# A 1-core attention and squared-ReLU FFN kernel: six blocks of weights stored whole and split later, and the engine order of c21 and c22 in the joint blocks

## Chip, core and metric

The kernel runs on one core of a Trainium2 chip. The metric is the device time of one execution in microseconds (us), the median over the runs shown. The engines are called by the profile's names: PE (TensorE), PEld (its weight loads), DVE (VectorE), ACT (ScalarE), POOL (GpSimd), SP (SyncE, which issues nearly all DMAs here).

## The reference, cut to what matters

```python
# attention, 8 x 8 heads, 576 rows, head_dim 64
q_s = softmax of q over its last axis;  k_s = softmax of k over the sequence
kv  = einsum('bhsd,bhde...', k_s, v);   attn = einsum(q_s, kv)
x   = attn.transpose(0, 2, 1, 3).reshape(4608, 512)
h   = np.maximum(x @ w_in, 0.0)          # w_in  512 x 2048
out = (h * h) @ w_out                    # w_out 2048 x 512
```

The FFN is most of the work. Its operands are split into a high and a low fp32r part, and each product is made of three matmuls (high x high, high x low, low x high).

## The kernel before, in words

The 4608 rows are nine tiles of 512 columns of x. Tiles 0 to 4 are the main part: for each of 16 slices f of w_in a first product, relu and square, a split, and a second product two slices later. The attention of later batches runs between them.

The last four tiles are done as two **joint blocks** (k = 0 and 1) of two tiles each, by a Strassen-Winograd scheme with seven products where there would be eight. `first_products(k)` loops over n = 0..7, the eight pairs of w_in slices. Each pair of slices is four quadrants a11, a12, a21, a22 of 128 x 256 values per k-half, and the scheme also needs four sums: s1 = a21 + a22, s2 = s1 - a11, s3 = a11 - a21, s4 = a12 - s2. PE does, for pair n, in this order: P1 (a11) into bank A, P2 (a12) into bank B, then P4 (a22) and P3 (s4) of the pair before (`old`), then P6 (s2) into A, P5 (s1) into B, P7 (s3) into A. Each of these is six matmuls. The two banks alternate between two sets from pair to pair, so P1 of pair n+1 writes the bank that P4 of pair n-1 filled.

What follows each product: u1 (a copy of A by ACT) after P1; c11 = B + u1, relu and square (DVE) after P2; c21 = relu and square of A (ACT) after P4; c12 = B + u2 (DVE), relu and square (ACT) after P3; u2 (ACT) after P6; u3 (ACT) after P7 and then c22 = B + u3 (DVE), relu and square (ACT in the kernel before). The four c go to DRAM (`g_b`), 256 KB each, and come back as operands of `second_products(k)`.

The weights of pair n+1 lie in one of two places, used in turn (`w` for even n, `ring` for odd n). Pairs 0 and 1 are loaded from DRAM with their sums (`w_sums`, high and low parts, 256 KB for each of the seven blocks). For pairs 2 to 7 (`OWN` = 2) the kernel before loads a11, a12 and a22 as high and low parts (three loads of 256 KB by `load_weights`) and beside them `own_a` (512 KB: a22 and a21, high and low), and `own_sums(n, w, step)` makes the four sums on DVE and splits them, in six steps spread over pair n-1. For pair 2 `own_a` is two tiles, own_k and own_q. In the main part `begin_sums(j)` stores the parts of these pairs to `w_sums` straight from where they lie (four DMAs of 256 KB per pair).

The order of the instructions in the joint blocks is that of the code; every engine and the SP queue take theirs in that order. In joint block 1 SP also carries the stores of block 0's output (`out_dram<-o`, four pieces of 64 KB in 128-byte rows each, after a 32 x 32 transpose on DVE). Their tiles o and the tiles of c21 share one pool tag, "gh", with two buffers.

Of the kernel before, what the change touches and what calls it, by code (L numbers as in the profile page):

```python
# [10 lines left out]
F32 = mybir.dt.float32  # L11
# [4 lines left out]
AF = mybir.ActivationFunctionType  # L16
ALU = mybir.AluOpType
# [319 lines left out]
def attention_ffn(  # L337
# [784 lines left out]

    def begin_sums(j):

        one, two = slabs[2 * j], slabs[2 * j + 1]
        for at, slab, cols in (
            (2, one, slice(0, HM)), (6, one, slice(HM, M)), (10, two, slice(HM, M)),
            (12, two, slice(0, HM)),
        )[:3 if j < OWN else 4]:
            Y.dma_start(out=w_sums[j][:, at:at + 2, :], in_=slab[:, :, cols].bitcast(F32))  # L1130

    def sums_by(key):

# [82 lines left out]

    def load_weights(n, w, *names):

        for name in names if w else ():
            if n >= OWN and name in SUMS:  # L1220
                continue
            at = SOURCE[name]
            Y.dma_start(out=w[name].bitcast(F32), in_=w_sums[n][:, at:at + 2, :])

    def own_sums(n, w, step):

        if n < OWN or n >= PAIRS:
            return
        if step == 0:
            if n == OWN:  # L1230
                a = [att.tile([P, 2, HM], F32, tag=tag, name=f"own_{tag}_{n}") for tag in "kq"]
                for i, one in enumerate(a):
                    Y.dma_start(out=one, in_=w_sums[n][:, 10 + 2 * i:12 + 2 * i, :])
            else:
                a = cvt.tile([P, 4, HM], F32, tag="w", name=f"own_a_{n}")
                Y.dma_start(out=a, in_=w_sums[n][:, 10:14, :])
            made["own", n] = [a]
            return
        if step == 1:
            made["own", n] += [cvt.tile([P, 4, HM], F32, tag="w", name=f"own_s_{n}")]  # L1240
        a, s = made["own", n]

        def two(name):
            return w[name][:, 0, :], w[name][:, 1, :]

        def split(name, of):
            S.copy(out=two(name)[0], in_=of)

        def rest(name, of):
            hi, lo = two(name)  # L1250
            V.tensor_tensor(out=lo, in0=of, in1=hi, op=ALU.subtract)

        def put(out, in0, op, in1):
            V.tensor_tensor(out=out, in0=in0, in1=in1, op=op)

        if n == OWN:
            a22, a11, a21, a12 = (a[i // 2][:, i % 2, :] for i in range(4))
        else:
            a22, a11, a21, a12 = (a[:, i, :] for i in range(4))
        s2, s3, s4 = (s[:, i, :] for i in range(3))  # L1260
        if step == 1 and n == OWN:
            put(a22, a22, ALU.add, a11)
            put(a21, a21, ALU.add, a12)
        elif step == 1:
            put(a[:, 0:4:2, :], a[:, 0:4:2, :], ALU.add, a[:, 1:4:2, :])
        elif step == 2 and n == OWN:
            for i, one in enumerate((a11, a12)):
                put(one, w["all"][:, 2 + 4 * i, :], ALU.add, w["all"][:, 3 + 4 * i, :])
        elif step == 2:
            put(a[:, 1:4:2, :], w["all"][:, 2:8:4, :], ALU.add, w["all"][:, 3:8:4, :])  # L1270
        elif step == 3:
            put(a22, a22, ALU.add, a21)
            split("s1", a22)
            if n == OWN:
                put(s2, a22, ALU.subtract, a11)
                put(s3, a11, ALU.subtract, a21)
            else:
                put(s[:, 0:2, :], a[:, 0:2, :], ALU.subtract, a[:, 1:3, :])
        elif step == 4:
            put(s4, a12, ALU.subtract, s2)  # L1280
            rest("s1", a22)
        elif step == 5:
            for name, of in (("s2", s2), ("s3", s3), ("s4", s4)):
                split(name, of)
            rest("s2", s2)
        elif step == 6:
            rest("s3", s3)
            rest("s4", s4)
# [264 lines left out]
    def sums_step(t, f):  # L1553

        j, i = divmod(f, NF // 2)
        j += 2 * (t - 1)
        if t >= 1 and j < NF // 2 and i == 3:
            begin_sums(j)
        for key, at in SUMS_AT.get(t, ()):
            for work, when in zip((full_sums, all_sums, rest_sums), at):  # L1560
                if f == when and f:
                    work(key)
# [16 lines left out]

    THRICE = (0, 0, 2), (4, 5, 7), (9, 10, 12)  # L1580
    SUMS_AT = {t: list(zip(KEYS[3 * t - 3:3 * t], THRICE)) for t in range(1, WT)}
    assert len(KEYS) <= 3 * (WT - 1)

    x_of, w_of, now = {}, {}, {"k": 0}
    ON_POOL = (
# [177 lines left out]
    def pair_p7(z):  # L1763
        product(z.A, z.w["s3"], x_of["t3"], False)
        u3 = temp("xh3", f"u3_{z.n}")
        S.copy(out=u3, in_=z.A)
        c = temp("ek", f"c22_{z.n}", att, 2)
        V.tensor_tensor(out=c, in0=z.B, in1=u3, op=ALU.add)
        own_sums(z.n + 1, w_of.get(z.n + 1), 5)
        S.activation(out=c, in_=c, func=AF.Relu)  # L1770
        square(c, S)
        keep("b21", z.n, c)

    def pair_p4(z):
        product(z.A, z.w["a22"], x_of["t4"], False)
        c = ffn.tile([P, M], F32, tag="gh", name=f"c21_{z.n}")
        S.activation(out=c, in_=z.A, func=AF.Relu)
        square(c, S)
        keep("b22", z.n, c)
# [196 lines left out]
    def first_products(k):  # L1976

        old = None
        for n in range(PAIRS):
            if n == 0 and k == 0:  # L1980
                split_x_of("t4")
                unit(3)
            elif n == 0:
                begin_ring()
            z = pair_begin(n)
            pair_p1(z)
            if n != 1 and turned_late:
                turned_late.pop(0)()
            if n == PAIRS - 1:
                load_raw("b11", 1, raw_place("b11"))  # L1990
            own_sums(n, z.w, 6)
            pair_p2(z)
            if n == 0 and turned_late:
                turned_late.pop(0)()
            if n == PAIRS - 1 and k == 0:
                full_sums(late_key)
            if n == 0 and k == 0:
                unit(2)
                begin_ring()
            elif n == 0:  # L2000
                split_x_of("t4")
                split_x_of("b22")
            if old:
                pair_p4(old)
                load_weights(n + 1, w_of.get(n + 1), "a22")
                own_sums(n + 1, w_of.get(n + 1), 1)
                pair_p3(old)
                load_weights(n + 1, w_of.get(n + 1), "s4")
            own_sums(n + 1, w_of.get(n + 1), 2)
            if n == PAIRS - 1:  # L2010
                load_raw("b11", 2, raw_place("b21"))
                split_step(0)
            pair_p6(z)
            if old:
                pair_c12(old)
            own_sums(n + 1, w_of.get(n + 1), 3)
            if n == 0:
                unit(3)
            pair_p5(z)
            own_sums(n + 1, w_of.get(n + 1), 4)  # L2020
            if n:
                own_sums(n + 2, None, 0)
            if n + 2 < PAIRS:
                w_of[n + 2] = weights(n + 2)
                load_weights(n + 2, w_of[n + 2], "a11", "a12", "s2", "s1")
            elif n == PAIRS - 1:
                if k == 0:
                    for i in range(4):
                        add_sums(late_key, i)
                load_raw("b21", 0, raw_place("t2"))  # L2030
                load_raw("b21", 1, raw_place("t2", 1))
                raw_x = att.tile([P, 4, M], F32, tag="x_next", name=f"raw_b12_{k}")
                for j in range(2):
                    load_raw("b12", j, raw_x[:, 2 * j:2 * j + 2, :])
                split_step(1)
            pair_p7(z)
            load_weights(n + 2, w_of.get(n + 2), "s3")
            if n == PAIRS - 3:
                load_raw("b11", 0, *(temp("v", f"raw_b11_{k}_{i}", att, 2) for i in range(2)))
            for j in FIRST_S[k].get(n, ()):  # L2040
                load_s("s1", j)
            if n == PAIRS - 1:
                for j in range(2):
                    load_raw("b22", j, raw_place("t3", j))
            old = z
        return old

    def second_products(k, old):
# [15 lines left out]
        for m in range(2):  # L2064
            product_step(0, m)
        pair_p4(old)
        load_raw("b12", 2, temp("k", f"raw_b12_{k}_4", att), temp("q", f"raw_b12_{k}_5", att))
        pair_p3(old)
        split_step(3)
# [127 lines left out]
```

## Time and profile before

| what | us |
|---|---|
| median of 3 runs | 837.98 |
| the three runs | 839.4, 836.86, 837.98 |
| the profiled execution | 836.44 |
| its span, first to last instruction | 834.7 |
| PE busy | 819.8 (98%) |
| DVE, ACT, POOL busy | 606.1, 494.6, 139.0 |
| granted TensorE clock, mean | 1.000 |

The table is read like this: PE is busy for all but 14.9 us of the span. The profile's start and end, before the first product and behind the last one, hold most of that; the rest is in single gaps.

### The profile page before, as it was taken

To read this page: it belongs to the slowest core of one execution; us is meant where nothing else is said; L and a number is where in the kernel's file an instruction comes from. 1 tells how busy PE (TensorE), PEld (TensorE's weight loads), DVE (VectorE), ACT (ScalarE), POOL (GpSimd) and SP (SyncE) were. 2 spreads that over 40 slices of the span, in tenths; PEclk is the share of its full clock that TensorE was granted. 3 is DMA by queue.
4 is the path that set the end of the run, shared out by engine and by line. 5 is a ranking of instruction groups with operands and counts; after the bars stand their busy time and mean duration, and the time that the engine had idled before them with its cause. 6 is when DMAs were issued, how large, how long until landed. Compare 5 with 4: busy or idle time off the path is not lost.

```text
span 834.7 us, 12955 instructions
## 1 busy us (share of the span) xinstructions
PE 819.8 (98%) x4411; PEld 663.3 (79%) x4411; DVE 606.1 (73%) x1100; ACT 494.6 (59%) x890; POOL 139.0 (17%) x151
## 2 busy tenths in 40 slices
PE   8999999999999999999999999999999999999997
PEld 7677777888878888888888888888888877787886
DVE  6988976877667755867555775567799966765995
ACT  5988844565655554655555656567744555675442
POOL 5889990001001000001000000000300000000000
PEclk9999999999999999999999999999999999999999
DMA  9993114536436555555637353998866688989455
GB/s 281 371 345 120 39 27 134 134 105 166 109 110 161 132 198 132 163 158 142 168 120 193 69 159 121 313 318 288 326 211 199 184 253 279 272 281 387 133 177 98
DMA packets 230146, 158.08 MB, mean 189 GB/s; under 512 B 147392, under 2 KB 200128, under 8 KB 230080
## 3 DMA queue, kind: packets, MB, share of 16 engines
q1 hardware_dynamic: 224160, 155.55, 61.1%
q10 hardware_dynamic: 5920, 1.71, 0.9%
q8 instruction: 35, 0.57, 0.3%
q14 instruction: 31, 0.25, 0.1%
HBM read 106.95 MB, written 49.81 MB: 188 GB/s over the span
## 4 chain that ended last, share of the span: by engine, by line
PE 80%; DMA 10%; DVE 4%; SPq 3%; ACT 2%; issue 1%; POOL 0%; DVEq 0%; ACTq 0%; POOLq 0%
PE acc L100 24%; PE h L100 21%; PE out L1866 16%; PE h L1315 13%; SPq L100 3%; DMA ring<-w_sums 2%; PE h_kv L100 2%; DMA raw<-in_moe_w_out_dram 2%; DMA k<-in_k_dram 2%; PE x L100 2%; DMA out_dram<-o 1%; DMA w<-g_b 1%; DMA own_a<-w_sums 1%; ACT r L100 1%; DVE w L100 0%
## 5 line engine op out<-in xcount | busy, mean ns | idle before, releaser
L100 PE MATMUL h<-xh,w 128*128 128x512 f32 x632 | 208.6, 392 | 1.0 <-ACT xh L100 0.8
L100 PE MATMUL acc<-w,gh 128*128 128x512 f32 x632 | 197.0, 393 | 0.0
L1866 PE MATMUL out<-w,w 128*128 128x512 f32 x636 | 148.9, 389 | 0.0
L100 PEld LDWEIGHTS h<-xh,w 128*128 128x128 f32 x632 | 118.6, 188 | 27.8 <-ACT xh L100 1.3
L1866 PEld LDWEIGHTS out<-w,w 128*128 128x128 f32 x636 | 119.2, 188 | 25.2 <-DVE w L100 0.4
L100 PEld LDWEIGHTS acc<-w,gh 128*128 128x128 f32 x632 | 117.0, 188 | 25.9 <-issue 1.7
L100 PE MATMUL acc<-w,gl 128*128 128x512 f32 x316 | 123.1, 390 | 0.0
L100 PE MATMUL h<-xl,w 128*128 128x512 f32 x316 | 123.1, 389 | 0.0
L100 DVE TENSOR_TENSOR gl<-r,gh 128x512 fp32r<-128x512 f32 x64 | 44.1, 688 | 82.3 <-ACT gh L100 82.0
L100 ACT ACTIVATE r<-h 128x512 f32<-128x512 f32 x79 | 47.1, 597 | 87.5 <-PE h L100 87.4
L100 POOL PARTITION_ALL_REDUCE kmx<-km x24 | 22.4, 933 | 340.8 <-DVE km L100 340.8
L1315 PE MATMUL h<-w,w 128*128 128x512 f32 x288 | 69.9, 391 | 1.3 <-DMA w<-w_sums 1.3
L100 PEld LDWEIGHTS h<-xl,w 128*128 128x128 f32 x316 | 59.4, 188 | 12.5 <-DVE xl L100 0.4
L100 PEld LDWEIGHTS acc<-w,gl 128*128 128x128 f32 x316 | 59.3, 188 | 12.5
L1315 PEld LDWEIGHTS h<-w,w 128*128 128x128 f32 x288 | 53.7, 188 | 14.0 <-DMA w<-w_sums 2.2
L100 ACT ACTIVATE c<-c 128x512 f32<-128x512 f32 x76 | 48.1, 633 | 19.5 <-DVE c L100 17.9
L100 ACT CAST gh<-r 128x512 fp32r<-128x512 f32 x64 | 39.5, 617 | 21.3 <-PE acc L100 20.8
L100 ACT CAST w<-w 128x1024 fp32r<-128x1024 f32 (+1 forms) x38 | 38.0, 1004 | 18.2 <-PE out L1866 8.6
L1315 PE MATMUL h<-w,ring 128*128 128x512 f32 x192 | 46.7, 391 | 0.4 <-DMA ring<-w_sums 0.4
L100 DVE TENSOR_TENSOR c<-h,u 128x512 f32<-128x512 f32 x48 | 33.0, 687 | 16.9 <-ACT u L100 13.7
L1315 PEld LDWEIGHTS h<-w,ring 128*128 128x128 f32 x192 | 35.8, 188 | 8.9 <-DMA ring<-w_sums 0.6
L100 POOL TENSOR_TENSOR w<-w,raw 128x512 int32<-128x512 int32 x32 | 41.8, 1326 | 1.7 <-DVE w L100 1.1
(238 smaller groups left out, 1266.1 us busy)
## 6 DMA issues: line engine op xcount, KB each, us to landing
w<-wo_sums SPq DMA_DIRECT2D x64, 256.0 KB, 3.4
g_b<-c SPq DMA_DIRECT2D x60, 256.0 KB, 4.4
w<-g_b SPq DMA_DIRECT2D x18, 512.0 KB, 7.1
raw<-in_moe_w_in_dram SPq DMA_DIRECT2D x16, 512.0 KB, 8.2
raw<-in_moe_w_out_dram SPq DMA_DIRECT2D x16, 512.0 KB, 8.8
w<-w_sums SPq DMA_DIRECT2D x32, 256.0 KB, 4.9
w_sums<-w SPq DMA_DIRECT2D x30, 256.0 KB, 2.7
v<-in_v_dram SPq DMA_DIRECT2D x56, 128.0 KB, 2.9
```

What stands on the lines that cost most here:

```text
L100: getattr(self.eng, op)(*map(real, args), **{k: real(a) for k, a in kwargs.items()})
L1315: nc.tensor.matmul(out=out.real(), lhsT=a[:, k * P:(k + 1) * P].real(), rhs=m[k].real(), start=(begin and k == 0 and i == 0), stop=(k == 1 ...
L1866: nc.tensor.matmul(out=banks[name][m].real(), lhsT=a[:, m * P:(m + 1) * P].real(), rhs=b[:, i, :].real(), start=fresh and j == i == k == 0 ...
```

## The change

Three things are changed.

1. For pairs 2 to 7 the main part now adds high and low parts on DVE (`full_sums`, two adds of 128 x 512 per pair) and `whole_sums` stores the sum, the whole float32 values of the four quadrants, with one DMA of 512 KB. In the joint blocks only `own_a` (512 KB: a11, a12 | a21, a22) is loaded; a11, a12 and a22 are split there, a11 and a12 in one ACT cast and one DVE subtraction (step 3), a22 with s1 (step 4). The four sums are made in steps 1 and 2, behind P3.
2. c22's relu and square is one DVE instruction (`SCALAR_TENSOR_TENSOR`) where it was two on ACT, and stands ahead of step 5's splits.
3. `pair_c21` is cut off `pair_p4` and stands behind u2 (behind P6 of the next pair); in the last pair `split_step(1)` stands behind P7 and its u3.

```diff
+    def whole_sums(j):
+        full_sums(("i", j))
+        whole = made.pop(("full", ("i", j)))
+        Y.dma_start(out=w_sums[j][:, 0:4, :], in_=whole.rearrange("p i (c n) -> p (i c) n", n=HM))
...
-        for name in names if w else ():
-            if n >= OWN and name in SUMS:
-                continue
+        for name in names if w and n < OWN else ():
...
-                a = cvt.tile([P, 4, HM], F32, tag="w", name=f"own_a_{n}")
-                Y.dma_start(out=a, in_=w_sums[n][:, 10:14, :])
+                whole = cvt.tile([P, 4, HM], F32, tag="w", name=f"own_a_{n}")
+                Y.dma_start(out=whole, in_=w_sums[n][:, 0:4, :])
...
+        if step == 1:
+            put(s1, a21, ALU.add, a22)
         elif step == 2:
+            put(s2, s1, ALU.subtract, a11)
+            put(s3, a11, ALU.subtract, a21)
+            put(s4, a12, ALU.subtract, s2)
         elif step == 3:
+            S.copy(out=two[0], in_=row)
+            put(two[1], row, ALU.subtract, two[0])
         elif step == 4:
+            split("s1", s1)
+            split("a22", a22)
+            rest("s1", s1)
+            rest("a22", a22)
...
+    WHOLE_AT = {1: [(2, 14)], 2: [(3, 14)], 3: [(4, 14)], 4: [(5, 2), (6, 4), (7, 5)]}
...
         V.tensor_tensor(out=c, in0=z.B, in1=u3, op=ALU.add)
+        square(c, V)
+        keep("b21", z.n, c)
         own_sums(z.n + 1, w_of.get(z.n + 1), 5)
-        S.activation(out=c, in_=c, func=AF.Relu)
-        square(c, S)
-        keep("b21", z.n, c)
...
             pair_p6(z)
+            own_sums(n + 1, w_of.get(n + 1), 3)
             if old:
+                pair_c21(old)
                 pair_c12(old)
-            own_sums(n + 1, w_of.get(n + 1), 3)
...
-                split_step(1)
-            pair_p7(z)
+            pair_p7(z)
+            if n == PAIRS - 1:
+                split_step(1)
```

The order of PE's and POOL's instructions is the same in both kernels. On the engines that PE waits for it changes at three kinds of places.

ACT in joint block 1, from u1 of pair 1 on (u1_1, u2_1, u3_1: the copies of pair 1; c21_0, c12_0: results of pair 0; own_k, own_q: the values of pair 2; w0, w13: where pair 2's weights go). Before:

```order
L100 COPY u1_1_6931<-h_1_0_6924 128x512
L100 ACTIVATE c21_0_6950<-h_0_0_6851 128x512
L100 ACTIVATE c21_0_6950<-c21_0_6950 128x512
L100 COPY u2_1_6973<-h_1_0_6924 128x512
L100 ACTIVATE c12_0_6963<-c12_0_6963 128x512 x2
L100 CAST w0_543<-own_k_2_6847 128x256
L100 COPY u3_1_7002<-h_1_0_6924 128x512
```

The same place in the changed kernel:

```order
L100 COPY u1_1_6917<-h_1_0_6910 128x512
L100 COPY u2_1_6955<-h_1_0_6910 128x512
L100 CAST w0_543<-own_k_2_6836 128x2x256
L100 ACTIVATE c21_0_6959<-h_0_0_6840 128x512
L100 ACTIVATE c21_0_6959<-c21_0_6959 128x512
L100 ACTIVATE c12_0_6942<-c12_0_6942 128x512 x2
L100 CAST w0_543<-own_s_2_6944 128x256
L100 CAST w13_1461<-own_q_2_6838 128x256
L100 COPY u3_1_6984<-h_1_0_6910 128x512
```

The copy u2 now stands ahead of c21, a cast of a11 and a12 stands between them, and u3 has one more 512-wide cast, one more 256-wide cast and c21 between itself and u2.

SP's queue in joint block 1, from the load of pair 4's values to the load of pair 5's (g1_*: stores of c; out_0_dram: stores of block 0's output). Before:

```order
L100 DMA own_a_4_7088<-w_sums_4_154 128x1024
L100 DMA w0_543<-w_sums_4_154 128x512 x2
L100 DMA g1_b21_1_121<-c22_2_7100 128x512
L100 DMA out_0_dram<-o_6_2_7120 32x16x32 x4
L100 DMA g1_b12_1_125<-c11_3_7135 128x512
L100 DMA g1_b22_1_129<-c21_2_7145 128x512
L100 DMA w13_1461<-w_sums_4_154 128x512
L100 DMA g1_b11_1_117<-c12_2_7157 128x512
L100 DMA own_a_5_7183<-w_sums_5_155 128x1024
```

The same place in the changed kernel:

```order
L100 DMA own_a_4_7072<-w_sums_4_154 128x1024
L100 DMA g1_b21_1_121<-c22_2_7082 128x512
L100 DMA out_0_dram<-o_6_2_7101 32x16x32 x4
L100 DMA g1_b12_1_125<-c11_3_7116 128x512
L100 DMA g1_b22_1_129<-c21_2_7149 128x512
L100 DMA g1_b11_1_117<-c12_2_7132 128x512
L100 DMA own_a_5_7166<-w_sums_5_155 128x1024
```

The three loads of w0 and w13 (a11, a12, a22) are gone, and nothing else moved here.

ACT at the end of the first products of joint block 1 (raw_b11 and w9: operands of the second products that come by DMA; w13: the high part made from w9). Before:

```order
L100 COPY u2_7_7535<-h_7_0_7483 128x512
L100 ACTIVATE c12_6_7522<-c12_6_7522 128x512 x2
L100 CAST w13_1461<-w9_1203 128x1024
L100 COPY u3_7_7558<-h_7_0_7483 128x512
L100 ACTIVATE c22_7_7560<-c22_7_7560 128x512 x2
```

The same place in the changed kernel:

```order
L100 COPY u2_7_7510<-h_7_0_7462 128x512
L100 ACTIVATE c21_6_7512<-h_6_0_7372 128x512
L100 ACTIVATE c21_6_7512<-c21_6_7512 128x512
L100 ACTIVATE c12_6_7497<-c12_6_7497 128x512 x2
L100 COPY u3_7_7535<-h_7_0_7462 128x512
L100 CAST w13_1461<-w9_1203 128x1024
```

The copy u3 now stands ahead of the cast that waits for a DMA, and c22's two instructions are gone from ACT.

## Rows read from the trace of the kernel before

**Rows 1.** The page: busy time by engine; groups (line, count, busy us, mean ns).
```profile
PE 819.8 (98%) x4411; PEld 663.3 (79%) x4411; DVE 606.1 (73%) x1100; ACT 494.6 (59%) x890; POOL 139.0 (17%) x151
...
L100 ACT CAST gh<-r 128x512 fp32r<-128x512 f32 x64 | 39.5, 617 | 21.3 <-PE acc L100 20.8
```

**Rows 2.** Waits of PE, both joint blocks (515 to 835 us): total us, times, longest.
```profile
PE h L1315 <- ACT u L100: 2.6, 2, 1.5
PE h L1315 <- DMA w<-w_sums: 1.3, 2, 0.9
PE h L1315 <- DMA ring<-w_sums: 0.4, 2, 0.2
```

**Rows 3.** Timeline of PE, joint block 0: start us, length us; P1 of two pairs.
```profile
553.94 2.88 PE L1315 MATMUL h<-w,w 128*128 128x512 f32 x12
...
563.46 2.88 PE L1315 MATMUL h<-w,ring 128*128 128x512 f32 x12
```

**Rows 4.** Timeline of PE, joint block 1: start, length, idle before and its releaser.
```profile
677.86 2.88 PE L1315 MATMUL h<-w,ring 128*128 128x512 f32 x12
...
687.27 1.66 PE L1315 MATMUL h<-w,ring_s 128*128 128x512 f32 x6 [1.09 <-ACT u L100]
689.40 3.03 PE L1315 MATMUL h<-w,w 128*128 128x512 f32 x12 [0.47 <-DMA w<-w_sums]
...
749.16 2.88 PE L1866 MATMUL out<-w,w 128*128 128x512 f32 x12
753.59 0.50 PE L1315 MATMUL h<-t4h,ring_a 128*128 128x512 f32 x1 [1.55 <-ACT u L100]
...
756.46 8.78 PE L1866 MATMUL out<-w,w 128*128 128x512 f32 x38
```

**Rows 5.** Timeline of ACT, joint block 1: what it waited for ahead of u2 and u3.
```profile
685.48 0.60 ACT L100 ACTIVATE c<-h 128x512 f32<-128x512 f32 x1 [4.31 <-DMA out_dram<-o]
...
752.00 1.04 ACT L100 CAST w<-w 128x1024 fp32r<-128x1024 f32 x1 [3.58 <-DMA w<-g_b]
```

**Rows 6.** DMA, 525 to 592 and 671 to 750 us: packets, MB, share; KB, us to landing.
```profile
q1 hardware_dynamic: 10914, 20.03, 87.9%
...
w<-w_sums SPq DMA_DIRECT2D x9, 256.0 KB, 5.2
...
q1 hardware_dynamic: 21438, 21.21, 88.1%
```

**Rows 7.** Tile own_a: its ten loads' time to landing; one wait of DVE, block 1.
```profile
DMA to landing us min/median/max: 3.6/5.5/7.5
...
708.99 0.69 DVE L100 TENSOR_TENSOR own_a<-own_a 128x512 f32<-128x512 f32 x1 [3.36 <-DMA own_a<-w_sums]
```

**Rows 8.** Timeline of ACT over one pair of joint block 0.
```profile
554.62 1.02 ACT L100 CAST w<-own_s 128x256 fp32r<-128x256 f32 x3
555.54 1.30 ACT L100 ACTIVATE c<-c 128x512 f32<-128x512 f32 x2
556.75 0.57 ACT L100 COPY u<-h 128x512 f32<-128x512 f32 x1
...
560.94 0.59 ACT L100 COPY u<-h 128x512 f32<-128x512 f32 x1 [1.46 <-PE h L1315]
561.42 1.30 ACT L100 ACTIVATE c<-c 128x512 f32<-128x512 f32 x2
```

**Rows 9.** Timeline of DVE over the same pair.
```profile
554.01 0.43 DVE L100 TENSOR_TENSOR own_s<-own_a,own_s 128x256 f32<-128x256 f32 x1
554.35 0.42 DVE L100 TENSOR_TENSOR w<-own_a,w 128x256 fp32r<-128x256 f32 x1
...
558.07 0.69 DVE L100 SCALAR_TENSOR_TENSOR c<-c 128x512 f32<-128x512 f32 x1
```

**Rows 10.** Main part: one full_sums on the chain of waits; DVE's idle time in slice 14.
```profile
141.43 1.30 DVE full_i L100 x2
...
219.31 0.69 DVE L100 TENSOR_TENSOR gl<-r,gh 128x512 fp32r<-128x512 f32 x1 [0.91 <-ACT gh L100]
```

More of the change, by code (lines that the diff above doesn't have):

```diff
@@ L1123, in begin_sums @@
     def begin_sums(j):
+        if j >= OWN:
+            return
         one, two = slabs[2 * j], slabs[2 * j + 1]
@@ L1127, in begin_sums @@
             (2, one, slice(0, HM)), (6, one, slice(HM, M)), (10, two, slice(HM, M)),
-            (12, two, slice(0, HM)),
-        )[:3 if j < OWN else 4]:
+        ):
             Y.dma_start(out=w_sums[j][:, at:at + 2, :], in_=slab[:, :, cols].bitcast(F32))
+    def whole_sums(j):
+        full_sums(("i", j))
+        whole = made.pop(("full", ("i", j)))
+        Y.dma_start(out=w_sums[j][:, 0:4, :], in_=whole.rearrange("p i (c n) -> p (i c) n", n=HM))
     def sums_by(key):
@@ L1232, in own_sums @@
                 for i, one in enumerate(a):
-                    Y.dma_start(out=one, in_=w_sums[n][:, 10 + 2 * i:12 + 2 * i, :])
+                    Y.dma_start(out=one, in_=w_sums[n][:, 2 * i:2 * i + 2, :])
             else:
-                a = cvt.tile([P, 4, HM], F32, tag="w", name=f"own_a_{n}")
-                Y.dma_start(out=a, in_=w_sums[n][:, 10:14, :])
+                whole = cvt.tile([P, 4, HM], F32, tag="w", name=f"own_a_{n}")
+                Y.dma_start(out=whole, in_=w_sums[n][:, 0:4, :])
+                a = [whole[:, 2 * i:2 * i + 2, :] for i in range(2)]
             made["own", n] = [a]
@@ L1240, in own_sums @@
             made["own", n] += [cvt.tile([P, 4, HM], F32, tag="w", name=f"own_s_{n}")]
-        a, s = made["own", n]
-        def two(name):
-            return w[name][:, 0, :], w[name][:, 1, :]
+        (row, other), s = made["own", n]
+        a11, a12, a21, a22 = row[:, 0, :], row[:, 1, :], other[:, 0, :], other[:, 1, :]
+        s1, s2, s3, s4 = (s[:, i, :] for i in range(4))
+        two = w["all"][:, 2:8:4, :], w["all"][:, 3:8:4, :]
         def split(name, of):
-            S.copy(out=two(name)[0], in_=of)
+            S.copy(out=w[name][:, 0, :], in_=of)
@@ L1249, in rest @@
         def rest(name, of):
-            hi, lo = two(name)
-            V.tensor_tensor(out=lo, in0=of, in1=hi, op=ALU.subtract)
+            V.tensor_tensor(out=w[name][:, 1, :], in0=of, in1=w[name][:, 0, :], op=ALU.subtract)
         def put(out, in0, op, in1):
             V.tensor_tensor(out=out, in0=in0, in1=in1, op=op)
[L1256 to L1268, printed above, removed]
+        if step == 1:
+            put(s1, a21, ALU.add, a22)
@@ L1269, in own_sums @@
         elif step == 2:
-            put(a[:, 1:4:2, :], w["all"][:, 2:8:4, :], ALU.add, w["all"][:, 3:8:4, :])
+            put(s2, s1, ALU.subtract, a11)
+            put(s3, a11, ALU.subtract, a21)
+            put(s4, a12, ALU.subtract, s2)
         elif step == 3:
[L1272 to L1278, printed above, removed]
+            S.copy(out=two[0], in_=row)
@@ L1279, in own_sums @@
+            put(two[1], row, ALU.subtract, two[0])
         elif step == 4:
-            put(s4, a12, ALU.subtract, s2)
-            rest("s1", a22)
+            split("s1", s1)
+            split("a22", a22)
+            rest("s1", s1)
+            rest("a22", a22)
         elif step == 5:
@@ L1558, in sums_step @@
             begin_sums(j)
+        for j, at in WHOLE_AT.get(t, ()):
+            if f == at:
+                whole_sums(j)
         for key, at in SUMS_AT.get(t, ()):
@@ L1581, in attention_ffn @@
     SUMS_AT = {t: list(zip(KEYS[3 * t - 3:3 * t], THRICE)) for t in range(1, WT)}
-    assert len(KEYS) <= 3 * (WT - 1)
+    assert len(KEYS) <= 3 * (WT - 2)
+    WHOLE_AT = {1: [(2, 14)], 2: [(3, 14)], 3: [(4, 14)], 4: [(5, 2), (6, 4), (7, 5)]}
+    assert sorted(j for at in WHOLE_AT.values() for j, _ in at) == list(range(OWN, PAIRS))
     x_of, w_of, now = {}, {}, {"k": 0}
@@ L1768, in pair_p7, with pair_c21 @@
         V.tensor_tensor(out=c, in0=z.B, in1=u3, op=ALU.add)
+        square(c, V)
+        keep("b21", z.n, c)
         own_sums(z.n + 1, w_of.get(z.n + 1), 5)
-        S.activation(out=c, in_=c, func=AF.Relu)
-        square(c, S)
-        keep("b21", z.n, c)
     def pair_p4(z):
         product(z.A, z.w["a22"], x_of["t4"], False)
+    def pair_c21(z):
         c = ffn.tile([P, M], F32, tag="gh", name=f"c21_{z.n}")
@@ L2005, in first_products @@
                 load_weights(n + 1, w_of.get(n + 1), "a22")
-                own_sums(n + 1, w_of.get(n + 1), 1)
                 pair_p3(old)
                 load_weights(n + 1, w_of.get(n + 1), "s4")
+                own_sums(n + 1, w_of.get(n + 1), 1)
             own_sums(n + 1, w_of.get(n + 1), 2)
@@ L2066, in second_products @@
         pair_p4(old)
+        pair_c21(old)
         load_raw("b12", 2, temp("k", f"raw_b12_{k}_4", att), temp("q", f"raw_b12_{k}_5", att))
```

## The prediction

> **What bounds the kernel now.** I read the page first: PE is busy 819.8 us [rows 1] of a span of 834.7, so everything that is not PE's own work is 14.9 us. PE's instructions are the same in both kernels, so the change can only act on PE's gaps. Next I read who PE waits for in the joint blocks, where the change lies: ACT's u twice (2.6 us), loads of weights four times (1.7 us) [rows 2]. The third view is PE's timeline. In joint block 0 P1 of one pair starts 9.52 us after that of the pair before [rows 3], which is seven products of 1.36 us without a gap. In joint block 1 it isn't so. From P1 of pair 1 (677.86) to the end of P7 of pair 7 (749.16) there are seven pairs in 71.30 us [rows 4]; seven times 9.52 are 66.64, so 4.66 us are lost. From 749.16 to 756.46 there are 24 matmuls, which at 1.36 us for six take 5.44 us and took 7.30: another 1.86 us. So block 1 loses 6.5 us, and that is what there is to win; block 0 loses next to nothing, and the rest of the 14.9 us lies outside what is changed.
>
> **Where each loss comes from.** (a) At 687.27 P7 of pair 1 waited 1.09 us for u2 [rows 4]. ACT had c21 ahead of u2, and c21 waited 4.31 us, until 685.48, for an output store to free its buffer [rows 5]. (b) At 689.40 P1 of pair 2 waited for the load of a11 [rows 4]; together with the other loads of rows 2 that is a late DMA, and the DMA engines were 88% busy in this stretch [rows 6]. own_a took 5.5 us in the median and up to 7.5 to land, and DVE stood 3.36 us for one of them [rows 7]. What DVE does late, ACT does late, and u1 and u3 follow; so the pairs that show no named wait are longer than 9.52 us too. (a) and (b) make up the 4.66 us. (c) At 753.59 P4 of pair 7 waited 1.55 us for u3 [rows 4], since ACT had ahead of it a cast that waited for a DMA until 752.00 [rows 5].
>
> **What the change does to them.** For (a), u2 stands ahead of c21: P6 of pair 1 is done long before 687.27, so P7 need not wait. What is late next is c21 itself, whose bank P1 of pair 2 overwrites; its buffer comes free at 685.48, and its relu (0.60 us [rows 5]) is done before pair 2 begins at 677.86 + 9.52 = 687.38. For (c), u3 stands ahead of the cast. What is late next is that cast, which feeds the second step of the second products, 5.44 us behind 749.16, at 754.60. It takes 1.04 us from 752.00 [rows 5] and DVE's subtraction of the same width about as long, so it is ready at about 754.3: just in time. For (b), three loads of 256 KB for each of six pairs are gone from each block, 18 x 256 KB = 4.7 MB of the 20.0 and 21.2 MB in the two stretches [rows 6]. 88% busy becomes about 68%, as an estimate from those rows.
>
> **What the change adds.** Time t counts from P1 of a pair, in us; the next pair's P1 is at 9.52.
> - ACT. u2 starts at 560.94 - 553.94 = 7.00 [rows 3, 8], the next instruction 0.48 later [rows 8]. The cast of a11 and a12 (0.62 [rows 1]) runs at 7.48, and c21 and c12, two relu and square of 1.21 each (555.54 to 556.75 [rows 8]), from 8.1 to 10.5. The casts of s1 and a22 take 0.31 each (three in 0.92 [rows 8]); u3 starts at about 11.1 and ends at 11.7. P4 of this pair starts at 9.52 + 2.72 = 12.24. So u3 has half a microsecond left: covered, but barely.
> - DVE. c12 follows P3 (t = 5.44) and ends at 6.3. Four sums of 256, 0.34 apart (554.01 to 554.35 [rows 9]), then the low parts of a11 and a12 (512 wide, 0.69): done at 8.8 where the cast ends at 8.1. P1 needs them at its third matmul, t = 9.97. Per pair DVE gets three more instructions of 256 and one fewer of 512 (c22's new one counted): 3 x 0.34 - 0.69 = +0.3 us. ACT gets as much less (two relu and square go, two casts come: 1.21 - 0.62 - 0.31). Both cost nothing while the chain above holds.
> - The new deadline. own_a must now be there for P1 of the next pair. The DVE path (four sums, then the low parts: 2.1 us) must end by 9.97, so own_a must land by t = 7.8. Before, PE needed the loads of a11 only at 9.52, and own_a later still. When does it land? Its buffer comes free when DVE has the low part of a22, at about 11.5, which is t = 2.0 of the next pair. The ten loads took 3.6 to 7.5 us [rows 7], so it lands at 5.6 to 9.5; with the median of before at 7.5. I take 4.5 us, between the shortest and the median, since the loads that shared the engines are gone: t = 6.5, 1.3 us early.
> - Main part. Six pairs get two DVE adds, 1.30 us [rows 10], behind idle time of 0.9 us ahead of a split whose result PE needs two slices later [rows 10]. Between 0 and 6 x 0.4 = 2.4 us; I take 0.2, as two slices of matmuls cover it. The stores shrink from 1 MB to 512 KB per pair, which nobody waits for.
>
> A rule of the Trainium skill speaks against the smaller pieces: "VectorE: DVE Perf Modes", section "The TRN2 errata — SBUF-src ops pay a fixed extra latency per instruction", wants at least 512 elements per instruction, since each pays a fixed cost, and prices an fp32 tensor_tensor at (N + 151) / 0.96 ns. For 256 that is 0.42 us, as each of rows 9 lasts; but the rows start 0.34 apart. By the rule the added work is 0.6 us per pair and not 0.3, and own_a's deadline 7.5; the sum stays.
>
> **The sum.** Recovered: 6.5 us. Given back: 0.2 in the main part, and 0.5 for one late own_a, that of pair 3 in block 1, which is issued into the crowd of pair 1's loads (bounds: 0, and 1.1 if it takes the longest 7.5 us from t = 1.3 and is due at 7.7). So 5.8 us: the profiled execution would go from 836.4 to 830.6. It lies 1.5 us below the median of the runs, so the median goes from 838.0 to **832.2 us**.
>
> **Rivals.**
> 1. *Only the order pays* (a and c, not b). The freed DMA time does not bring own_a early enough, and the pairs of block 1 stay as long as they are. Gain: in (a) 1.09 and in (c) 1.86, 2.95 us: 835.0. For it speaks that own_a's path is a ring: landing, casts, a22's low part, next load. Against it: 4.7 MB fewer in the same stretch.
> 2. *Slower: the ring of own_a sets the pace.* From the cast at 7.48 to the next issue are 4.0 us, so a pair takes 4.0 + landing. Beyond 5.5 us of landing that is more than 9.52, and PE stands in both blocks, for five loads each. With 6.5 us it costs 10 x 1.0 = 10 us and 6.5 are won: 841.5. It decides against the change from a mean landing of 6.15 us on. The median of before is 5.5 [rows 7], uncomfortably near; what speaks against is again that a fifth of the traffic is gone.
> 3. *No change.* The gaps move: u2 no longer waits, but u3 (half a microsecond left) and the low parts of a11 do, and about as long: 838. "Perfetto Trace Analysis", section "Identifying Performance Opportunities", in the Trainium skill, says that a kernel improves by improving its most-contended engine, and this change takes nothing off PE. By that rule nothing is won; the page's 14.9 us without PE are what it leaves out, and the same section sends the reader to such gaps.
>
> **How the numbers follow.** A measurement of this kernel tells about 0.3%, 2.5 us, from no change: faster is below 835.5, slower above 840.5. Forecast 0.60 (its own range 830.0 to 834.5: 6.5 us recovered and a little noise, down to half of it given back), rival 1 0.15, rival 3 0.15, rival 2 0.10. Rival 1 lies just inside faster. So faster 0.75, same 0.15, slower 0.10. The range for 8 in 10 goes from 829.8 to 837.0: the forecast, rival 1 and the nearer part of rival 3.
>
> **What would show it.** In the profile after: P1 to P1 of 9.5 us in block 1 as in block 0; no wait for u2 at P7 of pair 1 and none of 1.5 us at P4 of pair 7; the loads `w<-w_sums` and `ring<-w_sums` gone for pairs 2 to 7 and the DMA share of both stretches near 70%; own_a landing in less than 5 us and DVE hardly waiting for it. Wrong it would be if PE waits for DVE's or ACT's `w` and `ring` at P1 (own_a late), if P4 waits for u3 (ACT's chain too long), or if in the main part PE waits for a split behind the new adds.

## The result, and the profile after

| what | before | after |
|---|---|---|
| median, us (6 runs each, same chip) | 838.69 | 831.36 |
| lowest to highest | 836.76 to 841.45 | 829.84 to 833.7 |
| the profiled execution, us | 836.44 | 830.97 |
| its span | 834.7 | 829.0 |

The changed kernel is faster: the ratio is 0.9912, with a 95% interval from 0.9886 to 0.9938. In a later series it measured 831.32 (10 runs) and 0.9927 [0.9905, 0.9949]. Forecast were 832.2 for the median and a fall of 5.8 us for the profiled execution, which fell by 5.5. The median fell by 7.3, since the profiled execution of before lies 2.2 us below its median and that of after 0.4.

The page of the changed kernel, busy time by engine (to be read against rows 1):

```profile
PE 816.2 (98%) x4411; PEld 662.5 (80%) x4411; DVE 620.5 (75%) x1134; ACT 481.7 (58%) x882; POOL 143.9 (17%) x151
```

PE has the same 4411 matmuls, and yet it is busy for 3.6 us less: a short stand between two matmuls counts as busy time on the page, so PE's losses are more than the 14.9 us without PE show. From 671.06 to 756.46, block 1's first products before, the loss of 6.52 us is 4.15 us of idle time and 2.37 us of such stretched rows, at a granted clock of 1.00. DVE is busy for 14 us more, ACT for 13 us less, and neither is what the time follows. PE's waits in both joint blocks (total us, times, longest), the counterpart of rows 2:

```profile
PE h L1308 <- DMA ring<-w_sums: 0.2, 1, 0.2
```

Of 4.3 us in six waits one of 0.2 us is left. PE's timeline in joint block 1, the counterpart of rows 4:

```profile
678.56 2.88 PE L1308 MATMUL h<-w,ring 128*128 128x512 f32 x12
...
686.72 1.52 PE L1308 MATMUL h<-w,ring_s 128*128 128x512 f32 x6
688.08 2.88 PE L1308 MATMUL h<-w,w 128*128 128x512 f32 x12
...
745.20 2.88 PE L1865 MATMUL out<-w,w 128*128 128x512 f32 x12
747.92 0.39 PE L1308 MATMUL h<-t4h,ring_a 128*128 128x512 f32 x1
...
750.64 9.68 PE L1865 MATMUL out<-w,w 128*128 128x512 f32 x42
```

No row carries an idle time. P1 of pair 2 starts 9.52 us after that of pair 1; from 678.56 to the end of P7 of pair 7 at 745.20 are 66.64 us, exactly seven times 9.52; and the 24 matmuls behind it take 5.44 us. The loss of block 1 in this sense (the *loss* from here on) was 4.66 us in the pairs and 1.86 at the end; both are 0.0. ACT at the two places of rows 5:

```profile
685.56 0.59 ACT L100 COPY u<-h 128x512 f32<-128x512 f32 x1 [4.85 <-PE h L1308]
686.04 0.62 ACT L100 CAST w<-own_k 128x512 fp32r<-128x512 f32 x1
686.56 0.60 ACT L100 ACTIVATE c<-h 128x512 f32<-128x512 f32 x1
...
689.52 0.58 ACT L100 COPY u<-h 128x512 f32<-128x512 f32 x1
...
745.52 0.57 ACT L100 COPY u<-h 128x512 f32<-128x512 f32 x1
746.06 1.05 ACT L100 CAST w<-w 128x1024 fp32r<-128x1024 f32 x1
747.91 1.05 ACT L100 CAST w<-w 128x1024 fp32r<-128x1024 f32 x1 [0.80 <-DMA w<-g_b]
```

u2 (685.56) starts as soon as PE is done, and c21 behind it (686.56) no longer waits for the output store. u3 of this pair ends at 690.10, 0.70 us ahead of P4 at 690.80. In the last pair u3 (745.52) stands ahead of the casts, of which the first no longer waits for its DMA either and the second waits 0.80 us. The DMA view, from 520 to 587 us and from 666 to 743 us (packets, MB, share; then KB and median us to landing), the counterpart of rows 6:

```profile
q1 hardware_dynamic: 8384, 14.95, 67.6%
...
g_b<-c SPq DMA_DIRECT2D x25, 256.0 KB, 2.2
own_a<-w_sums SPq DMA_DIRECT2D x5, 512.0 KB, 3.6
...
q1 hardware_dynamic: 21228, 17.19, 74.6%
...
g_b<-c SPq DMA_DIRECT2D x27, 256.0 KB, 2.5
own_a<-w_sums SPq DMA_DIRECT2D x5, 512.0 KB, 4.1
```

The window of block 1 begins 5.8 us ahead of the block here and with it in rows 6; from 671.7 to 750.7 us, the same 79 us of the block, the share is 76.9%. The ten loads of own_a, the counterpart of rows 7:

```profile
DMA to landing us min/median/max: 3.6/3.7/4.6
```

Where the 5.7 us of span came from: block 1's first product starts at 671.76 instead of 671.06 (0.7 later), loses 0.0 instead of 6.5, and what follows takes 78.4 instead of 78.2. Part of the 0.7 is one wait of the main part (idle time and its releaser in brackets):

```profile
468.87 0.69 PE L100 MATMUL h_kv<-v,ek 128*64 128x65 f32 x16 [0.50 <-ACT xt L100]
```

### The profile page after: what moved, and what is told of

It reads as the page before. It is cut to its first block, busy times and chain, and to the rows that moved or that the text cites. A ratio compares the mean times of both kernels' runs of the same rounds, so it can differ in the third digit from the quotient of the medians.

```text
span 829.0 us, 12870 instructions
## 1 busy us (share of the span) xinstructions
PE 816.2 (98%) x4411; PEld 662.5 (80%) x4411; DVE 620.5 (75%) x1134; ACT 481.7 (58%) x882; POOL 143.9 (17%) x151
## 4 chain that ended last, share of the span: by engine, by line
PE 84%; DMA 5%; SPq 4%; DVE 4%; ACT 2%; issue 1%; POOL 0%; DVEq 0%; ACTq 0%
PE acc L100 22%; PE h L100 20%; PE out L1865 18%; PE h L1308 17%; SPq L100 4%; PE h_kv L100 2%; PE x L100 2%; DMA k<-in_k_dram 1%; DMA qn<-in_k_dram 1%; DMA raw<-in_moe_w_out_dram 1%; DMA ring<-w_sums 1%; DVE bst L100 1%; ACT r L100 1%; DVE km L100 0%; DMA kt<-in_k_dram 0%
## 5 line engine op out<-in xcount | busy, mean ns | idle before, releaser
L100 POOL PARTITION_ALL_REDUCE kmx<-km x24 | 26.7, 1111 | 337.2 <-DVE km L100 337.2
L100 ACT COPY u<-h 128x512 f32<-128x512 f32 x48 | 28.0, 583 | 62.8 <-PE h L1308 62.7
L100 ACT CAST w<-w 128x1024 fp32r<-128x1024 f32 (+1 forms) x38 | 38.0, 1006 | 18.4 <-PE out L1865 8.7
```

What stands on the lines that cost most here:

```text
L100: getattr(self.eng, op)(*map(real, args), **{k: real(a) for k, a in kwargs.items()})
```

## The experiments

The question was which of the three parts brings the gain. The prediction gave 2.95 us to the order of ACT's instructions (a and c) and the rest to the lower traffic (b). In the table "idle, 60 to 500" is PE's idle time in that stretch of the main part, "loss, pairs" and "loss, end" are as above, and "rest" is the span behind the end of block 1's first products. A kernel with one run has no ratio. A ratio is not the quotient of the two medians: for the order alone that would be 836.75 / 837.93 = 0.9986.

| kernel | median, us (runs) | ratio [95%] | idle, 60 to 500 | loss, pairs | loss, end | rest |
|---|---|---|---|---|---|---|
| before | 837.9 to 839.4, by series | 1 | 0.76 | 4.66 | 1.86 | 78.2 |
| changed | 831.36 (6) | 0.9912 [0.9886, 0.9938] | 1.21 | 0.0 | 0.0 | 78.4 |
| changed, again | 831.32 (10) | 0.9927 [0.9905, 0.9949] | 0.67 | 0.0 | 0.0 | 79.8 |
| order alone | 836.75 (10) | 0.997 [0.9949, 0.9991] | 0.76 | 7.46 | 0.0 | 79.3 |
| c22 alone | 836.81 (10) | 0.9999 [0.9979, 1.0019] | 0.74 | 3.61 | 1.86 | 78.6 |
| order and c22 | 836.52 (10) | 0.9986 [0.9969, 1.0003] | 0.77 | 6.42 | 0.0 | 79.4 |
| whole weights alone | 832.81 (4) | 0.9934 [0.9917, 0.9952] | 0.75 | 0.82 | 0.14 | 79.3 |
| changed, c21 back | 832.22 (1) | | 0.66 | 1.43 | 0.0 | 78.3 |
| changed, split back | 830.33 (1) | | 0.67 | 0.0 | 0.48 | 78.3 |
| changed, c22 on ACT | 831.09 (4) | 0.9918 [0.9894, 0.9942] | 1.64 | 0.0 | 0.0 | 78.7 |
| changed, traffic back | 837.7 (10) | 0.9991 [0.9966, 1.0016] | 1.12 | 4.94 | 0.0 | 79.6 |
| changed, adds later | 831.82 (7) | 0.9927 [0.9905, 0.995] | 2.46 | 0.0 | 0.0 | 78.3 |

**The order alone.** To the kernel before, c21 behind u2 and the second step's split behind P7:

```diff
+    def pair_c21(z):
...
+                pair_c21(old)
                 pair_c12(old)
...
-                split_step(1)
             pair_p7(z)
+            if n == PAIRS - 1:
+                split_step(1)
...
         pair_p4(old)
+        pair_c21(old)
```

> The kernel before with the new order alone: c21 behind u2, and the last pair's split behind P7; weights are loaded as before and c22 stays on ACT. My theory (three separate losses): P7 of pair 1 and P4 of pair 7 of joint block 1 no longer wait, the late loads stay, so block 1's loss against 9.52 us per pair falls from 6.5 us to about 3.5 and the time by about 3.0 us (0.4%). Rival (the order is what pays): the whole gain of the changed kernel, 6 to 7 us. Rival (the whole weights are what pays): under 1 us.

Measured: 836.75 us, 0.997 of before: a gain of 0.8 to 4.3 us by the interval, at the edge of what can be told, where 3 us were expected. In its profile block 1 loses 7.46 us in the pairs. PE's waits in both joint blocks:

```profile
PE h L1315 <- DMA w<-w_sums: 3.5, 3, 1.9
PE h L1315 <- DVE c L100: 0.8, 1, 0.8
PE out L1868 <- DVE w L100: 0.8, 1, 0.8
```

And two rows of its timeline in block 1, then the stretch behind the first wait (us, PE busy, granted clock, DMA share, GB/s):

```profile
688.24 4.58 PE L1315 MATMUL h<-w,w 128*128 128x512 f32 x12 [1.94 <-DMA w<-w_sums]
...
731.37 2.99 PE L1315 MATMUL h<-w,w 128*128 128x512 f32 x12 [1.25 <-DMA w<-w_sums]
...
688.24:691.65 3.41, 3.41 (x8) 0.51 1.06 388
```

The waits for u2 and u3 are gone as asked. But P1 of pair 2 now stands 1.94 us for a11's load. In this kernel block 1 begins at 669.82, so P1 starts 18.42 us into it; before it was 689.40 - 671.06 = 18.34 [rows 4]. It starts when the load lands, whatever u2 does: the 1.09 us for u2 had only covered the larger part of a wait that was there anyway. The two kernels with c22 on DVE show the same: P1 of pair 2 starts 17.59 us into the block where P7 waited 0.31 us for u2, and 17.72 where it didn't wait. This load isn't late because it is slow. SP's queue in the kernel before:

```profile
686.02 0.93 SPq L100 DMA_DIRECT2D w<-w_sums  x2
```

It is issued 14.96 us into the block (15.05 in the order alone), behind two output stores in SP's queue, and P1 is due at 6.80 + 9.52 = 16.32; it lands in 3.3 us, where such loads take 5.2 in the median [rows 6].

Of the 7.46 us 1.70 are a lower clock. PE stood 1.94 us ahead of P1, and behind that the granted clock was 0.5 of full speed for 3.4 us, the lower of its two levels (1.2 GHz), so that these twelve matmuls took 4.58 us instead of 2.88. In the kernel before the same delay came as two shorter waits, and the clock stayed at 1.00. Without these 1.70 us the block loses 5.8 us, 0.8 less than the 6.5 before. At the end 1.86 us are won, and 0.8 of them come back as a wait for the second step's low part ("out <- DVE w").

**c22 alone.** To the kernel before:

```diff
         V.tensor_tensor(out=c, in0=z.B, in1=u3, op=ALU.add)
-        own_sums(z.n + 1, w_of.get(z.n + 1), 5)
-        S.activation(out=c, in_=c, func=AF.Relu)
-        square(c, S)
+        square(c, V)
         keep("b21", z.n, c)
+        own_sums(z.n + 1, w_of.get(z.n + 1), 5)
```

> The kernel before with c22's relu and square as one DVE instruction and nothing else. My theory: no change beyond 0.5 us, as neither engine's total holds PE; block 1's loss stays near 6.5 us. Rival (ACT's length is what makes u1 and u3 late): pairs 2 to 6 of joint block 1 become shorter, 1 to 2.5 us won.

Measured: no change that can be told (0.9999, within 0.2% either way). The wait for u3 is the same 1.55 us; that for u2 is 0.31 instead of 1.09, and block 1 loses 5.5 us in this profile. **Order and c22 together**, both of these diffs:

> The kernel before with the new order and c22 on DVE, but weights loaded as parts: all of the change but the whole weights. My theory: as the order alone, about 3.0 us less, with the late loads at P1 still there (1 to 1.5 us of named waits). Rival (the whole weights don't matter): 6 to 7 us, and no waits at P1.

Measured: 0.9986, a gain of at most 2.6 us where 3 were expected; the loss of block 1 is 6.4 us, nearly as much as before, at a granted clock of 1.00. If c22 does nothing here either, both intervals hold for the order: 0.8 to 2.6 us. The lower end rests on the first interval alone; the medians of the three kernels lie within 0.3 us of each other. The two profiles show 0.1 us in block 1 here, and 0.8 in the order alone without its lower clock; behind the block 0.7 and 0.8 us go again to the wait "out <- DVE w".

**The whole weights alone.** To the changed kernel:

```diff
-        square(c, V)
-        keep("b21", z.n, c)
         own_sums(z.n + 1, w_of.get(z.n + 1), 5)
+        S.activation(out=c, in_=c, func=AF.Relu)
+        square(c, S)
+        keep("b21", z.n, c)
...
+                pair_c21(old)
...
-                pair_c21(old)
...
-            pair_p7(z)
             if n == PAIRS - 1:
                 split_step(1)
+            pair_p7(z)
```

> The changed kernel with the old engine order: weights whole and split in the joint blocks, but c21 ahead of u2, the split ahead of P7 and c22 on ACT. My theory: the pairs of joint block 1 take 9.52 us, the loads of w and ring no longer hold P1, DMA share falls from 88% to about 70%, but P7 of pair 1 still waits about 1.1 us for u2 and P4 of pair 7 about 1.5 us for u3; the time falls by 2.5 to 3.5 us. Rival (the order is what pays): the time stays within 1 us, since c21, u2 and u3 are late as before. Rival (the whole weights are what pays): 6 to 7 us, with those two waits gone as well.

Measured: 832.81 us, 0.9934. c21 stands ahead of u2 and the cast ahead of u3 as before the change, and yet PE's waits in both joint blocks are these:

```profile
PE h L1308 <- ACT u L100: 0.5, 1, 0.5
PE out L1866 <- DVE w L100: 0.3, 1, 0.3
```

The loss is 0.96 instead of 6.52 us: with the whole weights alone 5.6 of the 6.5 are gone in this profile, and by the interval the time falls by 4.0 to 7.0 us, where 2.5 to 3.5 were expected. The waits for u2 and u3 of the kernel before were themselves late DMAs, the store that held c21's buffer and the load ahead of the cast [rows 5].

**The traffic put back.** The changed kernel with three more transfers of 256 KB per pair 2 to 7, from DRAM to a place in DRAM that nothing reads; all else is computed as it is:

```diff
...
+            if n >= OWN:
+                if name in EXTRA:
+                    at = 2 * EXTRA.index(name)
+                    Y.dma_start(
+                        out=extra[now["k"], n][:, at:at + 2, :], in_=w_sums[n][:, 0:2, :]
+                    )
+                continue
...
```

> The changed kernel with extra traffic that nothing needs: at the places in the SP queue where the kernel before loads a11, a12 and a22 of pairs 2 to 7, three copies of 256 KB from DRAM to DRAM. If the traffic itself is what cost (so that own_a, the output stores and the second products' operands land late): DMA share near 88 to 95%, own_a lands in over 5 us, P1 waits for the split of a11 on DVE or ACT, joint block 1 loses 3 to 7 us and block 0 some too; 3 to 8 us slower than the changed kernel. If it was that P1 waited for a load of its own: block loss under 1 us and within 1.5 us of the changed kernel.

Measured: 837.7 us, 0.9991: nothing is left of the gain. The DMA view from 671 to 750 us:

```profile
q1 hardware_dynamic: 21446, 21.27, 86.8%
...
g_b<-c SPq DMA_DIRECT2D x28, 256.0 KB, 4.6
...
own_a<-w_sums SPq DMA_DIRECT2D x5, 512.0 KB, 5.9
out_dram<-o SPq DMA_DIRECT2D x20, 64.0 KB, 4.8
```

Four rows of PE's timeline in block 1:

```profile
697.66 0.73 PE L1320 MATMUL h<-w,ring 128*128 128x512 f32 x2 [0.63 <-ACT ring L100]
699.20 2.56 PE L1320 MATMUL h<-w,ring 128*128 128x512 f32 x10 [0.81 <-DVE ring L100]
709.65 2.57 PE L1320 MATMUL h<-w,w 128*128 128x512 f32 x10 [0.31 <-DVE w L100]
719.64 2.56 PE L1320 MATMUL h<-w,ring 128*128 128x512 f32 x10 [0.17 <-DVE ring L100]
```

This is the deadline of the prediction, at its place: own_a lands late, the cast of a11 and a12 follows, and P1 stands for it at its third matmul, for the low part. The ten loads take 3.5 to 7.0 us, in the median 5.6. So the loss of 4.9 us is about as large as the one before, but it isn't that loss put back: it lies at P1 of pairs 3 to 6.

The three copies put back work for the DMA engines and, as the loads before, places in SP's queue. Both make own_a late. Its load for pair 3 in SP's queue, here and in the changed kernel:

```profile
690.62 0.46 SPq L100 DMA_DIRECT2D own_a<-w_sums  x1
...
689.45 0.38 SPq L100 DMA_DIRECT2D own_a<-w_sums  x1
```

Here it is issued 3.27 us behind P1 of pair 2 (687.35) and lands in 6.3 us, so at 9.6; in the changed kernel it is issued at 1.37 (P1 at 688.08) and lands in 4.1, at 5.5. By the prediction it was due at 7.8. With either delay alone it would have come at 7.4 or 7.7, just in time. The run shows that three more transfers per pair, which nothing reads, are enough to take the gain away; it does not part SP's queue from the DMA engines.

**Single parts of the order undone in the changed kernel.** c21 ahead of u2 again:

```diff
+                pair_c21(old)
...
-                pair_c21(old)
```

> The changed kernel with c21 put back ahead of u2; whole weights, c22 on DVE and the late split stay. What the runs so far say (the traffic sets how late c21's buffer is): P7 of pair 1 of joint block 1 waits 0.3 to 1.1 us for u2, and no other pair loses anything; joint block 1 loses 0.5 to 1.3 us. Rival (order doesn't matter once the loads are gone): no wait for u2 at all.

Measured: 832.22 us in one run, and a loss of 1.43 us in the pairs, where 0.5 to 1.3 were expected. ACT in this kernel, at the place of the first row 5:

```profile
686.05 0.60 ACT L100 ACTIVATE c<-h 128x512 f32<-128x512 f32 x1 [5.51 <-DMA out_dram<-o]
686.68 0.63 ACT L100 ACTIVATE c<-c 128x512 f32<-128x512 f32 x1
687.22 0.57 ACT L100 COPY u<-h 128x512 f32<-128x512 f32 x1
```

Here (a) is back with its full cause and stands alone: nothing else is late at P1 of pair 2 any more, so now the place of c21 is worth 1.1 to 1.4 us in this profile. The store frees c21's buffer 14.46 us into the block (686.05 - 671.59), where it was 14.42 before, so the smaller traffic did not bring this store forward here. In the whole weights alone, with the same place of c21, the wait for u2 was 0.5 us. **The split of the second step ahead of P7 again:**

```diff
-            pair_p7(z)
             if n == PAIRS - 1:
                 split_step(1)
+            pair_p7(z)
```

> The changed kernel with the split of the second step (`split_step(1)`) ahead of P7 of the last pair again, as before the change. Theory now (the late loads made the wait for u3 at the end of block 1; with the traffic gone the order is worth little there): the run from P7 of pair 7 to the second products loses under 0.3 us, block 1 loses under 0.5 us in all, and the time is 830 to 833 us. Rival (my prediction's step: the order itself takes the 1.86 us): P4 of pair 7 waits for u3 by about 1.5 us again and the time is 833 us or more.

Measured: 830.33 us in one run, and 0.48 us lost at the end instead of 1.86, where under 0.3 were expected, since the DMA of the cast ahead of u3 lands 1.4 us behind the end of P7 (745.62 and 744.18) and not 2.8 (752.00 and 749.16 [rows 4, 5]). **c22 on ACT again**, the first part of the diff of the whole weights alone, once in one run (828.95 us, a loss of 0.04) and once timed:

> The changed kernel with c22's relu and square back on ACT (two instructions of 1.2 us in all). If the half microsecond that u3 has left is all the room there is: P6 of a pair waits for u1, or P4 for u3, and joint blocks 0 and 1 lose 0.2 to 1 us per pair. If ACT still has room (my expectation, since the two instructions stand behind u3 and u1 is due only 5.44 us into the pair): no wait in any pair, block loss under 0.3 us.

> The changed kernel with c22's relu and square on ACT as before the change, timed. Theory (ACT has room in a pair, since nothing arrives late any more, and c22's move gives nothing): the same as the changed kernel of this call within 0.3%, 830 to 833 us, no wait in the pairs of block 1. Rival (the move is what keeps u3 in time): 1 us or more slower than the changed kernel, with waits of PE for u at P4.

Measured: 831.09 us, as fast as the changed kernel of the same series, without a wait in the pairs. c22's move isn't needed.

**The adds in the main part.** The 0.50 us at 468.87 stood behind an attention load (`qn`) which stood behind the new stores in SP's queue; by that theory two of the stores were put later:

```diff
-    WHOLE_AT = {1: [(2, 14)], 2: [(3, 14)], 3: [(4, 14)], 4: [(5, 2), (6, 4), (7, 5)]}
+    WHOLE_AT = {1: [(2, 14)], 2: [(3, 14)], 3: [(4, 14)], 4: [(5, 2), (6, 6), (7, 8)]}
```

> The changed kernel with the sums of pairs 6 and 7 made two and three slices later in the last tile of the main part (slices 6 and 8 in place of 4 and 5). In the changed kernel PE waits 0.50 us at 468.87 for a copy that ACT does late, because DVE waited 5.4 us for a load of k that stands in SP's queue behind two stores of 512 KB. Theory (the stores hold up that load): this wait goes, 0.5 us less than the changed kernel, and nothing else changes. Rival (DVE's two adds themselves): the wait stays or moves to the next group of attention products.

Measured: 831.82 us, the same; but the wait grew instead of going:

```profile
469.00 0.69 PE L100 MATMUL h_kv<-v,ek 128*64 128x65 f32 x16 [1.79 <-ACT xt L100]
```

The theory fell; its rival, that DVE's adds themselves are the delay, is not excluded. **The changed kernel again** was to show whether that wait is scatter:

> The changed kernel itself again, beside the one above on the same chip: 0.9% below the kernel before, as in its first runs, with block 1 free of idle time in the pairs. What is asked is the wait of PE for a split in the main part, 0.5 us in its first profile and none in that of the kernel that differs only in c21: theory that it is scatter from run to run: it will be between 0 and 0.6 us here.

Measured: the wait of 0.50 us isn't there. In the eight profiles with the main part as changed (without that of the later adds, 2.46) the idle time from 60 to 500 us is 0.66 to 1.64, on average 1.00; in the four with the old one it is 0.74 to 0.77. So the changed main part has about 0.2 us more idle time on average, though four of the eight lie no higher than the old ones. Why the wait comes in some executions and not in others is open.

## Why the prediction was right, and where its working was not

- **What there was to win** was read rightly: 6.5 us, all in block 1, all recovered. That only the 14.9 us without PE could shrink was not: 3.6 us of the 5.7 went out of PE's busy time, which fell from 819.8 to 816.2. The measure by the 9.52 us of a pair caught them, since it doesn't go by named idle time.
- **The new deadline** holds as worked out. Its buffer comes free at 2.0 as reckoned, and in block 1 four of the five loads are issued 2.05 us behind P1. own_a lands in 3.7 us (4.1 in block 1) and not in 4.5, so no load is late, and the 0.5 us of the sum is 0.0. u3 has 0.7 us left, where half a microsecond stood. The DMA share came to 67.6% in block 0 and about 75 to 77% in block 1, where about 68% stood for both.
- **The main part:** 0.2 us was taken; 0.2 on average over the profiles, 0.5 in the first, with a scatter as large as that.
- **The second step's cast, "just in time",** is that: PE's wait "out <- DVE w" is absent in the first profile of the changed kernel and 0.6 us in the second, and it is there, with 0.2 to 0.8 us, in four of the nine profiles that have the split behind P7.
- **Where the step failed** is the split of the 6.5 us. (a) and (c) were added up as 2.95 us that the order earns, and rival 1 was priced from them. The order alone earned 0.8 to 2.6 us by the times, and by its profiles 0.1 to 0.8 in block 1 without the lower clock and about as much lost again behind it, as (a) lay over a late load and part of (c) came back one step later. The whole weights alone recover 5.6 us in the profile, about 5 if u2 waits as long as with c21 put back. (b) was put down to the share of the DMA engines; the load of pair 2 was late by its place in SP's queue and landed in 3.3 us. The step took the wait that the profile names at a place for what its removal earns. The two gains overlap, and the sum came out because the change takes both waits away.
- **Rival 2** names a danger that is there: with the traffic put back PE stands for own_a. Its price does not hold. At 5.6 us of landing it gives 10 x 0.1 = 1 us, and the pairs of block 1 lost 4.9: own_a was also issued 0.6 to 2.3 us later than in the changed kernel, which a fixed 4.0 us from the cast to the issue leaves out. The change itself stays clear of it by landing in 3.7 us. **Rival 3** is out: the interval excludes no change. The section of the Trainium skill that was weighed there ("Perfetto Trace Analysis", section "Identifying Performance Opportunities") sends the reader, once the engine is known, to the gaps on it and to what they wait for. The trace agrees with that: 0.9% came with PE's 4411 matmuls untouched, out of its waits.
- **The price of small DVE pieces** is that of the rows: 256-wide sums follow each other 0.34 us apart in the changed kernel as in rows 9. DVE's timeline there, at pair 1 of block 1:

```profile
685.26 0.43 DVE L100 TENSOR_TENSOR own_s<-own_s,own_k 128x256 f32<-128x256 f32 x1
685.60 0.42 DVE L100 TENSOR_TENSOR own_s<-own_k,own_q 128x256 f32<-128x256 f32 x1
685.94 0.42 DVE L100 TENSOR_TENSOR own_s<-own_k,own_s 128x256 f32<-128x256 f32 x1
```

By the formula (N + 151) / 0.96 ns in the section "The TRN2 errata — SBUF-src ops pay a fixed extra latency per instruction" of "VectorE: DVE Perf Modes", in the Trainium skill, an estimate for each is 0.42 us; the trace agrees on how long each lasts, and they start closer together than that. No wait hung on the difference.

## What to carry to other kernels

A wait's length in a profile isn't what its removal earns: look at what would have been late behind it, here a load that landed 18.4 us into the block either way. Where waits for several engines all go back to transfers, and the DMA engines show a high share, try first to make the transfers fewer; here the place of c21 showed its worth only afterwards. When a load is late, look at when it was issued as well as at how long it took. Values that are kept in two parts can be moved whole and split at the end, if the engines that split have room and the load's landing leaves a margin to its first use.

## What was unexpected of the hardware

A transfer's landing time moved far more than the DMA share. In the first 79 us of block 1 the share went from 88.1% [rows 6] to 76.9%, and the ten loads of own_a (512 KB, both blocks) went from 5.5 us in the median [rows 7] to 3.7. With the traffic put back (86.8%) it was 5.6 again, and g_b's stores of 256 KB took 4.6 us where the changed kernel's took 2.5. A wait of PE can cost nearly twice its length: in the order alone 1.94 us of standing were followed by 3.4 us at a granted clock of 0.5, which took another 1.70. Two profiles of the same kernel start block 1 at 671.76 and 669.15; 1.4 of these 2.6 us are one wait near the start ("kmT <- DVE sm", 1.8 against 0.4 us). The 2.6 us are nearly half of the 5.7 us of span that the change gained, and why the working compares stretches and not spans.
